# One core, local plus downsampled attention feeding two expert layers: the first batch's attention in another order, other warm-up thresholds, other scatter costs in the build-time planner

## The chip, the cores and the metric

The kernel runs on one core of a Trainium2 chip. The core has five engines with instruction queues of their own, each worked off strictly in the order written: TensorE (PE; its weight loads, PEld, overlap its matmuls), VectorE (DVE), ScalarE (ACT), GpSimd (POOL) and SyncE (SP), which here only issues DMA transfers. The metric is the device time of one execution in microseconds (us), smaller is better. Engines meet through semaphores: an instruction at the head of a queue that waits for another engine holds up all that stands behind it.

## The reference

```python
# attention: q, k, v are (4 batches, 8 heads, 576 tokens, 64)
q_d = q.reshape(B, H, Sd, 4, D).mean(axis=3)      # k_d, v_d alike: 144 tokens
out_d = sm_attn(q_d, k_d, v_d)                    # softmax attention, downsampled
out_up = np.repeat(out_d, 4, axis=2)
mask = np.abs(pos[:, None] - pos[None, :]) < 4    # a band of 7 keys
out_local = softmax(where(mask, scale * q @ k.T, -1e9)) @ v
x = (out_up + out_local)                          # to (2304 tokens, 512)
# expert 1: 512 -> 2048 -> 512
h = x @ w_in; g = maximum(h, 0) + alpha * minimum(h, 0); x = g @ w_out
# expert 2: 512 -> 2048 -> 512
h = x @ w_in; g = where(h > 0, h, exp(minimum(h, 0)) - 1); y = g @ w_out
```

## The kernel before

**Work.** The eight heads of a batch are handled as four pairs (p = 0 to 3), and a batch's tokens as two halves (u = 0, 1) of 288. For batch 0 the local part is computed with dense matmuls over blocks of 64 queries by 70 keys: `th_dense(p, u)` adds the mask (`maskb,identb` on the PE), makes the scores (`qk,qk 64x70`), takes the row maximum (`Dmx`), exponentiates (`dP`), divides (`Dden`), transposes (`ident,dP`), multiplies by the values (`dP,vd`) and adds the downsampled part into the tile `x` (`p_add`). The downsampled part is a chain of its own: `th_pair(0, p)` sums q, k and v in fours on DVE and transposes the sums of v (`ident,qk`), and `th_da0(p)` makes the scores (`qk 72x144`), copies them out (`P<-bank`), takes the maximum (`dmx`), exponentiates (`P,dsum`), divides (`dsum`, then four `P<-P,dsum`), transposes (`ident,P`), multiplies by the values (`pt,qk`) and copies out (`od`).

Batches 1 to 3 go another way in their local part. For batch 1 (`th_S`, `th_soft0`, `th_p`) the scores are written to HBM (`scr<-ss`), read back along the diagonal (`s<-scr`, 72 x 32 runs of seven numbers), normalised to `a`, scattered back along the diagonal into a zeroed tensor (`pscr<-a`, pieces of 28 bytes), and read as a matrix (`pp<-pscr`), which the PE transposes (`ident,pp`) and multiplies by the values (`ppT,vb`).

**Experts.** Expert 1 walks 128 steps of one block of 128 hidden units for 288 tokens: first `mm_in` (`x,rawi` in plain fp32 for the first six steps, afterwards `xh,wi` and `xl,wi`, operands split in a high and a low part), two steps later `out1` (`r,rawo`, then `gh,wo`, `gl,wo`), whose results are evicted as `ys` and stored to HBM (`yT<-ys`). Weights come as 8-byte numbers and are decoded on ACT and DVE (`cp`, `cw`, `wi`, `wo`). Expert 2 works on blocks of 512 tokens with seven products in place of eight for a 2 by 2 split of the matrix.

**What sets the order.** The whole program is written while a planner in the kernel file runs along. Each piece of work is a generator (a thread); `spawn(thread, priority)` sorts the threads by priority, smaller first. `_Clock` keeps an assumed time of every engine and of the DMA queue. `cons()` lets the first thread go on whose next ACT, DVE or SP instruction could start about now by these times; `pe(budget)` does so for threads that want PE and free PSUM banks. The expert steps are written out in a fixed order, and attention matmuls are put between them by `tick()` and `fill()`. So a priority or an assumed cost changes nothing in what is computed: it changes which instruction stands before which, in the queue of every engine. In the first expert step the four parts of `mm_in` each wait for one pair's `x` (`run_until("xcp", kt)`).

**Warm-up matmuls.** While the planner waits, it puts in matmuls on a constant (`bank<-warm`), as long as it holds that the PE has done few columns lately: `_Clock.quiet()` compares the columns of the last four of its ticks with `WANT`.

**Names.** All instructions are recorded at one helper's line, L293 (before) or L298 (after), so a group is told by its tiles, not by its line.

Of the kernel before, what the change touches and what calls it, by code (L numbers as in the profile page):

```python
# [39 lines left out]
LAG = 2  # L40
SP_ = S + 2 * HALO
F1 = 6
G2 = 512
U2 = G2 // 2
XR = 11
# [43 lines left out]

class _Clock:  # L90
    TICK, KEEP, RISE, COLD = 2560 / 3, 2600.0, 3100.0, 12
    WANT = 4000.0, 3600.0
    LAG = {("ACT", "DVE"): 142.0, ("ACT", "PE"): 194.0, ("ACT", "SP"): 145.0, ("DVE", "ACT"): 128.0,
           ("DVE", "DVE"): 127.0, ("DVE", "PE"): 179.0, ("DVE", "SP"): 120.0, ("PE", "ACT"): 197.0,
           ("PE", "DVE"): 196.0, ("PE", "SP"): 189.0, ("DMA", "SP"): 900.0, ("DMA", "ACT"): 907.0,
# [3 lines left out]
    MANY = {"ACT": 70.0, "DVE": 93.0, "SP": 50.0, "PE": 0.0, "POOL": 90.0}  # L99

    def __init__(self):
        self.cols, self.gear = {}, []
        self.t = dict.fromkeys(("PE", "ACT", "DVE", "SP", "DMA", "POOL"), 0.0)
        self.t["SP"] = 560.0
        self.hw = 0.0
        self.ports = {"DVE": [], "POOL": []}
        self.seen = {}
        self.share = 1.0
        self.uses, self.bar, self.slots, self.count = {}, {}, {}, {}
        self.cur = self.ctx()  # L110
# [23 lines left out]

    def quiet(self):
        k = int(self.t["PE"] / self.TICK)
        return self.last(k) < self.WANT[self.fast(k)]

    def span(self, ap):
        dims = [(abs(int(a)), int(n)) for a, n in ap.ap]  # L140
# [82 lines left out]
    def dma(self, out, in_):  # L223
        outs, ins = [self.span(out)], [self.span(in_)]
        n = int(out.shape[0]) * _free(out) * (8 if out.dtype == U64 else 4)
        piece = min(self.run(out), self.run(in_))
        cost = max(n / 360 * (2 if piece < 512 else 1), n / piece / 16 * 7)
        self.t["SP"] = max(self.t["SP"], self.deps("SP", outs, ins))
        self.hw = max(self.hw + 25, self.t["SP"]) + 450
        end = max(self.t["DMA"], self.hw + 650) + cost  # L230
        self.t["DMA"] = end
        self.note("DMA", outs, ins, end)
        c = self.cur
        c["t"] = max(c["t"], end + 900)
        c["on"] = "DMA"
# [62 lines left out]
def fused_kernel(ctx: ExitStack, tc: tile.TileContext, qk, vt, vl, ql, kl, vb, w_in1, w_out1, alpha,  # L298
                 w_in2, w_out2, ident_d, mask_d, zero_d, vd, maskd_d, out):
    nc = tc.nc  # L300
    ck = _Clock()
# [1500 lines left out]
    with tc.manual_schedule():  # L1802
# [28 lines left out]
        put("vv")  # L1831
        put("vv")
        for p in range(NP):
            spawn(th_pair(0, p), -6 + p / 10)
            spawn(th_da0(p), -7 + p / 10)
            spawn(th_dense(p, 0), -9 + p / 10)
            spawn(th_dense(p, 1), US + p / 10, 0)
        spawn(th_ldw(), 0)
        for k in range(2 * NF):
# [29 lines left out]
        for s in range(NS1):  # L1869
# [36 lines left out]
            if not s:  # L1906
# [3 lines left out]
                for z in (1, 0):  # L1910
                    at(0.0)
                    SP.dma_start(out=pscr[z][0].rearrange("(q y) -> q y", y=RW + 1), in_=zero_d)
                slot[0] = 0
                spawn(th_x0(), -20)
            tm["mm", s] = ck.t["PE"]
            if s < F1:
# [125 lines left out]
```

## Time and profile before

| | |
|---|---|
| median of 3 runs | 939.83 us (933.84 to 940.98) |
| the profiled execution | 935.59 us |
| its span, first to last instruction | 933.7 us |
| outside the span | 1.9 us |
| busy in the span: PE, DVE, ACT, POOL | 97%, 77%, 56%, 0% |
| mean granted PE clock | 0.986 of full speed |

The profile comes from one execution. A busy PE is not a PE at its peak: its matmuls take twice as long while the granted clock is 0.5 (1.2 in place of 2.4 GHz). Idle time of an engine costs something only where the PE waits for it in the end, since the PE has by far the most work.

### The profile page before, as it was taken

What the parts mean: (1) busy time and instruction counts of PE and PEld (TensorE: products, weight loads), DVE (VectorE), ACT (ScalarE), POOL (GpSimd) and SP (SyncE); (2) the same over time, 40 slices, a digit from 0 to 9 for tenths busy, and PEclk for the clock granted to TensorE, in tenths of its full rate; (3) what the DMA queues carried; (4) which work ended last, traced back from release to release, by engine and by line L of the source; (5) the groups of instructions that cost most, each with busy time, mean ns of one, the idle gap of its engine ahead of it and who ended that gap; (6) DMA issues with size and microseconds to landing.
All of it is one profiled execution on the core that took longest, in us unless ns stands there. A gap on an engine that the chain in (4) does not pass through costs nothing.

```text
span 933.7 us, 17520 instructions
## 1 busy us (share of the span) xinstructions
PE 905.9 (97%) x6727; PEld 832.6 (89%) x6727; DVE 722.0 (77%) x1552; ACT 524.8 (56%) x1312; POOL 2.9 (0%) x6
## 2 busy tenths in 40 slices
PE   6899999899999999999999998999999999999998
PEld 4568998799999999999999997998989989899987
DVE  5788985436969899999536999998797659989753
ACT  5798786454444562323335676665566456756543
POOL 0000000000000000000100000000000000000000
PEclk8799999999999999999999999999999999999999
DMA  9676815414221423110203570524233243252502
GB/s 262 214 271 222 293 55 110 110 64 148 56 78 49 138 64 96 44 44 9 63 2 116 188 224 24 180 68 136 50 132 90 70 153 128 85 161 88 179 11 81
DMA packets 69417, 106.36 MB, mean 114 GB/s; under 512 B 26610, under 2 KB 43378, under 8 KB 69154
## 3 DMA queue, kind: packets, MB, share of 16 engines
q1 hardware_dynamic: 69334, 105.25, 36.3%
q8 instruction: 52, 0.85, 0.4%
q14 instruction: 31, 0.25, 0.1%
HBM read 86.89 MB, written 19.78 MB: 114 GB/s over the span
## 4 chain that ended last, share of the span: by engine, by line
PE 82%; DVE 6%; DMA 6%; ACT 4%; issue 2%; SPq 1%; DVEq 0%; ACTq 0%
PE bank L293 82%; DMA qk<-in_qk_dram 3%; DMA s<-scr 1%; SPq L293 1%; DMA pscr<-a 1%; DMA pp<-pscr 1%; DMA rawo<-in_w_out_dram 1%; DVE cw L293 1%; DVE gl L293 1%; ACT wo L293 1%; ACT n L293 1%; DVE wi L293 1%; DVE cp L293 0%; DVE r L293 0%; ACT dP L293 0%
## 5 line engine op out<-in xcount | busy, mean ns | idle before, releaser
L293 PE MATMUL bank<-gh,wo 128*128 128x288 f32 x976 | 223.7, 300 | 1.6 <-ACT ys L293 1.6
L293 PE MATMUL bank<-xh,wi 128*128 128x288 f32 x976 | 223.3, 300 | 0.0
L293 PEld LDWEIGHTS bank<-xq,wi 128*128 128x128 f32 x1536 | 195.6, 192 | 9.6 <-ACT wi L293 2.0
L293 PE MATMUL bank<-xq,wi 128*128 128x256 f32 x1536 | 198.1, 284 | 3.0 <-ACT wi L293 1.6
L293 ACT ACTIVATE n<-bank 128x288 f32<-128x288 f32 (+1 forms) x176 | 70.7, 402 | 200.1 <-PE bank L293 197.9
L293 PE MATMUL bank<-wo,gh 128*128 128x512 f32 x576 | 179.4, 393 | 0.1
L293 PEld LDWEIGHTS bank<-gh,wo 128*128 128x128 f32 x976 | 165.5, 188 | 5.8 <-issue 2.7
L293 PEld LDWEIGHTS bank<-xh,wi 128*128 128x128 f32 x976 | 164.8, 188 | 3.2 <-issue 1.7
L293 PE MATMUL bank<-gl,wo 128*128 128x288 f32 x488 | 144.7, 297 | 0.0
L293 PE MATMUL bank<-xl,wi 128*128 128x288 f32 x488 | 143.8, 295 | 0.1
L293 PEld LDWEIGHTS bank<-wo,gh 128*128 128x128 f32 x576 | 103.3, 189 | 17.8 <-ACT gh L293 0.3
L293 PE MATMUL bank<-wo,gl 128*128 128x512 f32 x288 | 112.3, 390 | 0.2 <-DVE gl L293 0.2
L293 DVE SCALAR_TENSOR_TENSOR r<-n,nal,bank 128x288 f32<-128x288 f32 x128 | 65.3, 510 | 53.6 <-ACT n L293 52.7
L293 PEld LDWEIGHTS bank<-xl,wi 128*128 128x128 f32 x488 | 92.0, 189 | 0.7 <-DVE xl L293 0.6
L293 PEld LDWEIGHTS bank<-gl,wo 128*128 128x128 f32 x488 | 91.9, 188 | 0.1
L293 ACT ACTIVATE gh<-r 128x288 fp32r<-128x288 f32 x122 | 54.0, 443 | 66.0 <-DVE r L293 65.9
L293 DVE TENSOR_TENSOR gl<-r,gh 128x288 fp32r<-128x288 f32 x122 | 55.5, 455 | 16.9 <-ACT gh L293 16.2
L293 PEld LDWEIGHTS bank<-wo,gl 128*128 128x128 f32 x288 | 54.1, 188 | 12.5 <-DVE gl L293 0.6
L293 DVE TENSOR_TENSOR gl<-n,gh 128x512 fp32r<-128x512 f32 (+1 forms) x80 | 50.5, 634 | 7.6 <-ACT gh L293 6.5
L293 DVE TENSOR_TENSOR c<-m,bank 128x256 f32<-128x256 f32 x64 | 26.7, 419 | 37.0 <-PE bank L293 36.6
L293 ACT ACTIVATE gh<-n 128x512 fp32r<-128x512 f32 (+1 forms) x80 | 46.3, 581 | 11.8 <-DVE n L293 11.6
L293 ACT ACTIVATE n<-n 128x512 f32<-128x512 f32 (+1 forms) x80 | 47.1, 589 | 2.5
(125 smaller groups left out, 1218.1 us busy)
## 6 DMA issues: line engine op xcount, KB each, us to landing
rawi<-in_w_in_dram SPq DMA_DIRECT2D x40, 512.0 KB
rawo<-in_w_out_dram SPq DMA_DIRECT2D x40, 512.0 KB
qk<-in_qk_dram SPq DMA_DIRECT2D x12, 582.0 KB
x<-yT SPq DMA_DIRECT2D x8, 576.0 KB
osp<-os SPq DMA_DIRECT2D x18, 256.0 KB
os<-osp SPq DMA_DIRECT2D x18, 256.0 KB
out_dram<-os SPq DMA_DIRECT2D x18, 256.0 KB
yT<-ys SPq DMA_DIRECT2D x28, 144.0 KB
```

The source lines that it names most:

```text
L293: return fn(*args, **kw)
```

## The change

The priorities of batch 0's first half are set by new numbers: within a pair the downsampled scores come first (-14.7), then the dense local part (-14.6), then sums and transposes (-13.3), and each pair stands a whole step of 1.0 after the one before it. Before, all four dense parts (-9) stood ahead of all four downsampled chains (-7), and these ahead of all sums (-6), a tenth apart by pair. Up to the end of the first expert step's `mm_in` the planner asks for 5600 and 5200 columns in place of 4000 and 3600 before it leaves out a warm-up matmul. And it takes a transfer in pieces under 64 bytes to cost 31 ns (into HBM) or 15 ns (else) for a piece and engine, in place of 7.

```diff
+VP = -13.3
+DP = -14.7
+NP0 = -14.6
+STEP = 1.0
...
-    WANT = 4000.0, 3600.0
+    WANT, HEAD = (4000.0, 3600.0), (5600.0, 5200.0)
...
-        return self.last(k) < self.WANT[self.fast(k)]
+        return self.last(k) < (self.HEAD if self.head else self.WANT)[self.fast(k)]
...
-        cost = max(n / 360 * (2 if piece < 512 else 1), n / piece / 16 * 7)
+        rate = 7 if piece >= 64 else 31 if out.space == bass.MemoryType.DRAM else 15
+        cost = max(n / 360 * (2 if piece < 512 else 1), n / piece / 16 * rate)
...
-            spawn(th_pair(0, p), -6 + p / 10)
-            spawn(th_da0(p), -7 + p / 10)
-            spawn(th_dense(p, 0), -9 + p / 10)
+            spawn(th_pair(0, p), VP + p * STEP)
+            spawn(th_da0(p), DP + p * STEP)
+            spawn(th_dense(p, 0), NP0 + p * STEP)
...
                 slot[0] = 0
+                ck.head = False
                 spawn(th_x0(), -20)
```

No instruction is added or taken away on ACT, DVE, POOL and SP; on the PE the warm-up matmuls go from 27 to 21 (17 ahead of the first score and 10 between the pairs, now 18 and 3). All else is order. Three places show it.

The PE's queue after the second pair's dense scores, before the change. `dP_188`, `dP_220` and `dP_245` are the probabilities of the dense parts of pairs 0, 1 and 2; `qk_31` is pair 3.

```order
L293 MATMUL bank_73<-ident,dP_188 70x128 x4
L293 MATMUL bank_66<-ident,dP_188 70x128
L293 LDWEIGHTS identb
L293 MATMUL bank_67<-maskb,identb 128x350
L293 MATMUL bank_67<-qk_31_133,qk_30_132 64x70 x10
L293 LDWEIGHTS identb
L293 MATMUL bank_67<-maskb,identb 128x350
L293 MATMUL bank_68<-ident,dP_220 70x128 x4
L293 MATMUL bank_69<-ident,dP_220 70x128
L293 MATMUL bank_73<-ident,dP_245 70x128 x4
L293 MATMUL bank_66<-ident,dP_245 70x128
L293 MATMUL bank_72<-qk_11_117 72x144
```

The same place now; `qk_01` and `qk_11` carry the sums of pairs 0 and 1, `dP_189` and `dP_236` the dense parts of pairs 0 and 1.

```order
L298 MATMUL bank_72<-qk_11_117 72x144
L298 MATMUL bank_73<-qk_11_117 72x144
L298 MATMUL bank_67<-ident,qk_01_108 72x128 x2
L298 LDWEIGHTS identb
L298 MATMUL bank_68<-maskb,identb 128x350
L298 MATMUL bank_68<-qk_21_125,qk_20_124 64x70 x10
L298 LDWEIGHTS identb
L298 MATMUL bank_68<-maskb,identb 128x350
L298 MATMUL bank_66<-ident,P 72x72 x4
L298 MATMUL bank_72<-ident,P 72x72 x4
L298 MATMUL bank_73<-ident,dP_189 70x128 x4
L298 MATMUL bank_69<-ident,dP_189 70x128
```

Pair 1's downsampled scores (`qk_11_117`) and pair 0's downsampled transposes (`ident,P`) moved ahead of the dense work of pairs 2 and 3.

The end of this stage on the PE, before: from the last product but one of the downsampled chains to the end of the first expert step's four parts (`x,rawi`, three and one).

```order
L293 MATMUL bank_68<-pt,qk_20_124 64x144 x4
L293 MATMUL bank_67<-ident,P 72x72 x4
L293 MATMUL bank_73<-ident,P 72x72 x4
L293 MATMUL bank_66<-dP_245,vd_138 64x64 x8
L293 MATMUL bank_66<-dP_245,vd_138 64x32 x2
L293 MATMUL bank_69<-pt,qk_30_132 64x144 x4
L293 MATMUL bank_70<-x,rawi_280 128x288 x3
L293 MATMUL bank_72<-dP_291,vd_140 64x64 x8
L293 MATMUL bank_72<-dP_291,vd_140 64x32 x2
L293 MATMUL bank_70<-x,rawi_280 128x288
```

And now.

```order
L298 MATMUL bank_70<-x,rawi_275 128x288 x2
L298 MATMUL bank_66<-pt,qk_20_124 64x144 x4
L298 MATMUL bank_69<-ident,P 72x72 x4
L298 MATMUL bank_72<-ident,P 72x72 x4
L298 MATMUL bank_67<-ident,qk_31_133 72x128 x2
L298 MATMUL bank_68<-dP_299,vd_138 64x64 x8
L298 MATMUL bank_68<-dP_299,vd_138 64x32 x2
L298 MATMUL bank_73<-pt,qk_30_132 64x144 x4
L298 MATMUL bank_70<-x,rawi_275 128x288
L298 MATMUL bank_66<-dP_355,vd_140 64x64 x8
L298 MATMUL bank_66<-dP_355,vd_140 64x32 x2
L298 MATMUL bank_70<-x,rawi_275 128x288
```

The first two expert parts now stand ahead of pair 2's downsampled product; pair 3's chain still comes last.

SP's queue around batch 1's way through HBM, before. `pscr_96` and `pscr_97` are the scattered probabilities of the two halves.

```order
L293 DMA s_1876<-scr_0_94 72x32x7
L293 DMA scr_1_95<-ss 72x624
L293 DMA pscr_96<-a 72x32x7
L293 DMA yT_82<-ys 128x288 x2
L293 DMA s_1973<-scr_1_95 72x32x7
L293 DMA pp<-pscr_96 72x624 x2
L293 DMA yT_82<-ys 128x288 x2
L293 DMA qk<-in_qk_dram 128x1164
L293 DMA vv<-in_vt_dram 128x576
L293 DMA pp<-pscr_96 72x624
L293 DMA pscr_97<-a 72x32x7
L293 DMA pp<-pscr_96 72x624
```

And now.

```order
L298 DMA s_1874<-scr_0_94 72x32x7
L298 DMA scr_1_95<-ss 72x624
L298 DMA yT_82<-ys 128x288 x2
L298 DMA s_1969<-scr_1_95 72x32x7
L298 DMA pscr_96<-a 72x32x7
L298 DMA yT_82<-ys 128x288 x2
L298 DMA qk<-in_qk_dram 128x1164
L298 DMA vv<-in_vt_dram 128x576
L298 DMA pscr_97<-a 72x32x7
L298 DMA pp<-pscr_96 72x624 x2
L298 DMA qk<-in_qk_dram 128x1164
L298 DMA vv<-in_vt_dram 128x576
```

The first scatter moved behind the first two stores of `yT` and the second read of scores, and all reads of scattered probabilities moved behind the second scatter. In the PE's queue the first `ident,pp` moved from behind 486 expert matmuls to behind 564.

## Rows read from the trace of the kernel before

**Rows 1.** The page: the span, busy time of each engine.

```profile
span 933.7 us, 17520 instructions
PE 905.9 (97%) x6727; PEld 832.6 (89%) x6727; DVE 722.0 (77%) x1552; ACT 524.8 (56%) x1312; POOL 2.9 (0%) x6
```

**Rows 2.** The chain that ended last, 0 to 90 us: start, length, what.

```profile
29.19 0.67 DVE dmx L293
...
30.15 1.70 ACT P L293 x8
...
45.88 0.47 DVE x L293
...
46.40 22.34 PE bank L293 x200
```

**Rows 3.** Windows: PE, PEld, DVE, ACT, POOL busy; granted PE clock; DMA share, GB/s.

```profile
28.00:32.00 4.00, 1.75 (x20) 1.09 (x17) 3.08 (x11) 2.67 (x12) 0.00 (x0) 0.90 1.06 243
32.00:36.00 4.00, 3.81 (x37) 3.15 (x38) 1.95 (x8) 3.17 (x14) 0.00 (x0) 0.50 0.92 235
44.00:48.00 4.00, 3.44 (x47) 2.10 (x46) 3.14 (x8) 2.18 (x4) 0.00 (x0) 0.89 0.22 84
```

**Rows 4.** Waits of the PE, 46 to 130 us: for what, us in total, times, longest.

```profile
PE bank L293 <- DMA qk<-in_qk_dram: 1.6, 2, 0.9
PE bank L293 <- DMA rawo<-in_w_out_dram: 1.2, 1, 1.2
PE bank L293 <- DVE x L293: 0.6, 1, 0.6
```

**Rows 5.** The same, 130 to 300 us.

```profile
PE bank L293 <- DMA pp<-pscr: 3.0, 3, 1.7
PE bank L293 <- ACT ys L293: 1.6, 1, 1.6
```

**Rows 6.** The same, 490 to 580 us.

```profile
PE bank L293 <- ACT wi L293: 1.6, 1, 1.6
PE bank L293 <- DVE wi L293: 1.3, 1, 1.3
```

**Rows 7.** Timeline of the PE, 0 to 60 us: start, busy, operation, [idle before].

```profile
26.18 0.72 PE L293 MATMUL bank<-pt,qk 72*64 72x144 f32 x8
...
29.60 0.72 PE L293 MATMUL bank<-qk 64*72 64x144 f32 x8
32.20 1.51 PE L293 MATMUL bank<-pt,qk 72*64 72x144 f32 x8 [1.88 <-ACT pt L293]
...
36.75 1.24 PE L293 MATMUL bank<-pt,qk 72*64 72x144 f32 x8
37.91 1.18 PE L293 MATMUL bank<-ident,P 72*72 72x72 f32 x8
39.02 1.28 PE L293 MATMUL bank<-dP,vd 70*64 70x64 f32 x20
...
41.99 3.14 PE L293 MATMUL bank<-x,rawi 128*128 128x288 f32 x6 [0.66 <-DVE rawi L293]
```

**Rows 8.** The chain that ended last, 130 to 185 us.

```profile
152.00 5.19 DMA s<-scr
...
160.57 7.51 DMA pscr<-a
...
168.16 5.86 DMA pp<-pscr
```

**Rows 9.** Timeline of ACT, 130 to 185 us.

```profile
156.00 0.71 ACT L293 ACTIVATE ys<-bank 128x288 f32<-128x288 f32 x2 [2.24 <-DMA yT<-ys]
```

**Rows 10.** Timeline of the PE, 128 to 185 us.

```profile
158.43 0.70 PE L293 MATMUL bank<-ident,pp 72*78 72x72 f32 x8
```

**Rows 11.** Timeline of SP's queue, 130 to 185 us.

```profile
149.22 0.30 SPq L293 DMA_DIRECT2D pscr<-a  x1
151.01 0.82 SPq L293 DMA_DIRECT2D yT<-ys  x2
```

More of the change, by code (lines that the diff above doesn't have):

```diff
@@ L101, in __init__ @@
     def __init__(self):
-        self.cols, self.gear = {}, []
+        self.cols, self.gear, self.head = {}, [], True
         self.t = dict.fromkeys(("PE", "ACT", "DVE", "SP", "DMA", "POOL"), 0.0)
```

## The prediction

> **What bounds the kernel now.** First the page's busy times: the PE works 905.9 of 933.7 us [rows 1], so all but 27.8 us of the span is PE work that this change doesn't touch, and only the idle time of the PE and its time at half clock can be won. Then the chain that ended last, for the place of both. In the first 46 us it runs over loads, DVE and ACT; from 46.40 it is 22.34 us of PE without a break [rows 2]. So everything ahead of 46.40, the start of the last part of the first expert step, is a lead that the whole kernel pays. Then the windows for the clock: from 32 to 36 the PE is busy 3.81 of 4.00 us, but at a granted clock of 0.50, 1.2 in place of 2.4 GHz. The mean of 0.90 in 28 to 32 puts the fall at 31.2, and the 0.89 in 44 to 48 the rise at 44.9 [rows 3]. Last the PE's waits behind the lead, by what ended them: 3.4 us from 46 to 130 [rows 4], 4.6 from 130 to 300 [rows 5], 2.9 from 490 to 580 [rows 6]. The sum is made against the profiled execution's 935.59, of which 1.9 lies outside the span. It is one of the lower of the four times shown; the median lies 4.2 higher.
>
> **The lead.** ACT, DVE and the PE do the same work in both kernels, apart from warm-ups, and the first loads come in the same order. What changes is what still has to run when the last pair's probabilities are ready. Before, four dense parts went first and the downsampled chains came one after another, so that their transposes and products piled up behind 32.2 and ran at half clock. Now pairs 0 and 1 are through before pair 2's chain begins. I walked the new queues by hand, with the durations of the rows. Pair 2's exponentials stand on ACT behind pair 3's dense ones and the copies for pair 1, and start at an estimated 28.4 (30.15 before), taking 1.70 [rows 2]. Behind them come two pairs of copies (0.65 each), the maximum (0.67 [rows 2], 1.2 with its scaling and hops) and pair 3's exponentials, which so end at an estimated 35.1; two more copies make it 36.2. From there the PE has, at half clock, a product `pt,qk` (1.24), transposes `ident,P` (1.18), the transposes of v's sums (an estimated 0.64), `dP,vd` (1.28), `pt,qk` (1.24), one expert part (3.14 / 6 = 0.52) and `dP,vd` (1.28) [rows 7]: 7.4, so 43.6. The last add (0.47 [rows 2]) and two hops of 0.15 put the last part of the first expert step at 44.4, 2.0 ahead of 46.40.
>
> Against it stands the clock. In the kernel before it rose at 44.9, 2.9 us after the expert parts had begun in a row at 41.99 [rows 7], and so ahead of the unbroken stretch. Now two parts run early, between small matmuls, and the dense stretch begins only at 44.4. If it takes the clock 2.9 us again, 1.45 us of work are lost there. Net I take **0.6**. Upward: a fall only at 31.2, as before, would by the same walk give 43.3, so 3.1 - 1.5 = 1.6; no fall at all is a rival below. Downward: the walk sums some thirty short instructions and may be 2 off, so -1.4.
>
> Will it fall? The planner now wants more columns, but sees fewer gaps in its own order and puts in 3 warm-ups between the pairs, not 10. My walk leaves the PE idle for about 2 us near 25 (for the copy `pt` of pair 1 behind the dense exponentials) and 1.5 near 30. Before, it had been idle only since 30.3 (29.60 + 0.72) when the clock fell at 31.2 [rows 3, 7], among the same small matmuls. That is the nearest row, so I take it that the clock falls between 24 and 28. The Trainium skill, page "TensorE: Matmul & The Clock Gate", section "Why this matters for your kernels", speaks for the other side: it asks only that no long idle gaps stand between bursts of matmuls, and by that the clock would hold here. The trace doesn't bear it out for this mix, since 0.9 us of idle time was enough. By the rule the sum would be that of the first rival.
>
> **From 46 to 130.** The loads of batch 1's q and k stand one place earlier on SP, and the score matmuls of its second pair now stand behind 126 expert matmuls, not 105. Of the 1.6 us that the PE waited for `qk` [rows 4] I take **1.0** as won. The waits for `rawo` and `x` lose no cause. The bounds are all 3.4, and -2.2: one weight load of 512 KB slips behind the stores of `yT0a`, into a stretch with fuller queues, and takes 2.2 at the 243 GB/s of [rows 3]; ACT and DVE decode at high load there, but that weight (block 10 of `w_in`) is needed only in the eleventh step of the next group, which hides it. Without that cover the 2.2 would be paid.
>
> **From 130 to 300.** Two causes. First, the stores of `ys`: the first scatter was issued at 149.22 and the first two stores at 151.01 [rows 11] went behind it, so ACT waited 2.24 for a free `ys` tile until 156.00 [rows 9], and the PE 1.6 for a bank [rows 5]. Now the stores stand ahead of the scatter: 1.6 is won. Second, the reads `pp`: the PE waited 3.0 for them [rows 5]. The first transposes `ident,pp` stood at 158.43 [rows 10]. They now stand behind 78 more expert matmuls, at 905.9 / 6727 = 0.135 each [rows 1] 10.5 us, and some 1.5 us of other attention work moved ahead: 158.4 - 1.6 + 12.0 = 168.8 on the old scale. The price is that SP waits for the second half's probabilities before it issues any read. The second read `s` was issued at 152.00 and took 5.19 [rows 8] behind the first scatter; ahead of it, some 1.5 less. So the second scatter goes out near 159, not 160.57, and the first reads right behind. A scatter took 7.51, a read behind it or behind the loads of q, k and v 5.86 [rows 8]. If the scatter holds them up wholly, they land near 159 + 7.5 + 2 = 168.5, just in time. Each later read starts when a transpose frees its tile, 4 to 6 us ahead of its own turn. I take **4.0** of the 4.6 as won, with bounds of 0 and 4.6.
>
> The Trainium skill, page "DMA: Bandwidth & Descriptors", section "Queues, rings and completion order", says that an engine takes descriptors in ring order and that a transfer's completion is written only after all earlier writes of that engine. By it every read behind the second scatter is late; no row shows a read that overtook a scatter, and 5.86 fits. By the rule the sum would be that of the second rival, if later reads lose as much.
>
> **From 490 to 580.** DVE and ACT prepare `wo` earlier and some `wi` later by a place or two. It can take away the 2.9 us or double them [rows 6]; the moves go both ways, so I count 0. The remaining order differs between attention and expert work that the PE's queue hides.
>
> **Sum:** 0.6 + 1.0 + 4.0 = 5.6, and 935.6 - 5.6 = **930.0**.
>
> **Rivals.** *The clock holds* through the lead. Then the seven PE pieces shrink by 0.72 / 1.24 [rows 7], from 7.4 to 4.3, pair 3's scores come 1.1 earlier, and the last part starts at 40.5: 5.9 in place of 0.6, and 924.7. For it: the PE's gaps are filled better than before. Against it: seven warm-ups fewer, and the fall at 31.2 after less than a microsecond of idle time.
>
> *The reads stay late.* Each read lands 5.86 after its issue, behind scatter and loads, while its tile comes free only about 4 us ahead of its turn. Four such misses of 1 to 1.5 us eat up the 4.6: 935.6 - 0.6 - 1.0 = 934.0. For it: all reads now stand behind both scatters. Against it: they have 10 us more.
>
> *The low clock lasts* (the slower side). Behind 44.4 the PE alternates expert parts with the second half's dense scores. If this mix did not raise the clock, the 22.34 us stretch [rows 2] would run at half speed. Each low microsecond loses half of one; from 14 us on (14 / 2 = 2.0 + 1.0 + 4.0) the kernel is slower than before, and with the whole stretch it is 935.6 - 7.0 + 22.3 = 951. Against it: in 44 to 48 the same kinds of matmul held the full clock [rows 3].
>
> That the change doesn't do what its words say is true for the warm-ups (21, not more than 27), and lies in the forecast.
>
> **How the numbers follow.** Chances: forecast 0.45, clock holds 0.25, reads late 0.23, low clock lasts 0.07. The range: 922 takes in the first rival with 2.7 us of luck in the open terms; 938 takes in the second, with the 4.2 us by which the median of the runs lies over the profiled one. Only the third falls out, and tails. About 1%, 9.4 us, is what a measurement of this kernel can tell from no change. The forecast's gain of 5.6 stays within it, unless the open terms add 4 (a third of its 0.45); the first rival's 10.9 goes beyond. So faster 0.25 + 0.15 = 0.40, slower 0.06, within 0.54.
>
> **What would show it.** Right: the last `x,rawi` of the first step between 43 and 45; a clock of 0.50 from before 30 to about 47; no wait for `ys` and under 1 us for `pp`. Wrong in the lead: a clock of 1.00 from 20 on, and the last `x,rawi` by 41. Wrong in the middle: several waits for `pp` behind 168. The forecast fails altogether if the PE gains waits for `wi` near 560, or for weights before 130.

## The result and the profile after

The changed kernel takes 927.48 us (median of four runs, 925.15 to 928.21), the kernel before beside it 940.4. The ratio is 0.9875 with a 95% interval of 0.9838 to 0.9912, so the change makes the kernel 1.25% faster. The profiled execution took 928.21 us against a forecast of 930.0 and against 935.59 before; its span is 7.3 us shorter. By the medians the gain is 12.9 us, because the profiled execution of the kernel before was one of its shorter ones.

The page's head: the span and the busy times, to be held against [rows 1].

```profile
span 926.4 us, 17510 instructions
PE 903.6 (98%) x6721; PEld 831.4 (90%) x6721; DVE 721.1 (78%) x1552; ACT 523.3 (56%) x1312; POOL 2.9 (0%) x6
```

The PE's busy time fell by 2.3 us and its idle time by 5.0. Its timeline in the lead, with the idle time before each row in brackets, answers [rows 7].

```profile
22.08 0.46 PE L298 MATMUL bank<-qk 64*72 64x144 f32 x2
24.60 0.71 PE L298 MATMUL bank<-qk 64*72 64x144 f32 x6 [2.05 <-ACT od L298]
26.38 1.52 PE L298 MATMUL bank<-pt,qk 72*64 72x144 f32 x8 [1.07 <-ACT pt L298]
...
33.86 1.24 PE L298 MATMUL bank<-x,rawi 128*128 128x288 f32 x4 [0.24 <-DVE rawi L298]
35.92 0.72 PE L298 MATMUL bank<-pt,qk 72*64 72x144 f32 x8 [0.82 <-ACT qk L298]
...
38.90 0.75 PE L298 MATMUL bank<-x,rawi 128*128 128x288 f32 x2
39.58 0.78 PE L298 MATMUL bank<-dP,vd 70*64 70x64 f32 x20
41.39 0.75 PE L298 MATMUL bank<-x,rawi 128*128 128x288 f32 x2 [1.03 <-DVE x L298]
```

The last part of the first expert step starts at 41.39 us, 5.0 earlier than the 46.40 of [rows 2]. Two of its four parts already stand at 33.86. Two new waits of 2.05 and 1.07 us stand before 26.4, both for ACT. The windows of the same stretch (PE, PEld, DVE, ACT and POOL busy, granted clock, DMA share, GB/s) tell what they did to the clock, as [rows 3] did.

```profile
24.00:28.00 4.00, 2.33 (x15) 1.67 (x16) 1.68 (x6) 3.84 (x18) 0.00 (x0) 0.77 1.03 410
28.00:32.00 4.00, 4.00 (x36) 3.04 (x36) 3.19 (x11) 3.05 (x13) 0.00 (x0) 0.50 1.06 288
32.00:36.00 4.00, 2.94 (x20) 2.03 (x20) 2.52 (x9) 3.68 (x15) 0.00 (x0) 0.88 0.89 316
```

A mean of 0.77 puts the fall to half clock at 26.2, the 0.88 the rise at 33.0. So the low stretch, which lay on 31.2 to 44.9 before [rows 3], ends ahead of all expert parts. What ACT was doing while the PE stood shows in ACT's timeline.

```profile
20.42 0.40 ACT L298 ACTIVATE qk<-bank 72x256 f32<-72x256 f32 x1
23.70 0.66 ACT L298 ACTIVATE cp<-rawi 128x512 f32<-128x512 f32 x1 [2.89 <-DMA rawi<-in_w_in_dram]
24.27 0.28 ACT L298 ACTIVATE od<-bank 128x144 f32<-128x144 f32 x1
...
25.91 0.71 ACT L298 ACTIVATE pt<-bank 72x288 f32<-72x288 f32 x2
```

ACT stood 2.89 us at `cp`, the first step of decoding the first weight block, until that block had landed. The copy `od`, pair 3's dense exponentials and the copy `pt` queued behind it, and the PE waited for these.

In the middle the PE's waits from 130 to 300 us, the view of [rows 5], are nearly gone.

```profile
PE bank L298 <- DVE wi L298: 0.6, 1, 0.6
PE bank L298 <- DMA qk<-in_qk_dram: 0.3, 1, 0.3
```

The queue of SP around batch 1's way through HBM (start, time on the queue) and the first transposes of what it reads answer [rows 10, 11].

```profile
148.61 2.22 SPq L298 DMA_DIRECT2D pscr<-a  x1
150.88 2.20 SPq L298 DMA_DIRECT2D yT<-ys  x2
...
156.55 0.32 SPq L298 DMA_DIRECT2D pscr<-a  x1
157.24 3.02 SPq L298 DMA_DIRECT2D pp<-pscr  x2
```

```profile
165.96 0.67 PE L298 MATMUL bank<-ident,pp 72*78 72x72 f32 x8
167.31 0.69 PE L298 MATMUL bank<-ident,pp 72*78 72x72 f32 x8
```

The reads go out right behind the second scatter, 8.7 us ahead of their transposes, which start without a wait.

A ledger tells where the time came from. It takes the start of ACT's copy `n<-bank` of an expert step in the profiled execution of before (its start there is given), less the start of the same copy in another run. The runs e1 to e12 are those of the next section; the second column is the start of the last part of the first expert step (43.60 is read as the last `x,rawi` of that step), the third the stretch at half clock in the lead from 20 us on, worked out from the windows' means as above.

| run | last part | half clock | 47.2 | 148.5 | 291.6 | 464.4 | 866.2 |
|---|---|---|---|---|---|---|---|
| before | 46.40 | 31.2-44.9 | 0 | 0 | 0 | 0 | 0 |
| after | 41.39 | 26.2-33.0 | 4.2 | 3.9 | 9.1 | 9.1 | 7.2 |
| e1 | 41.77 | 23.7-33.9 | 3.8 | 3.4 | -3.3 | -3.7 | -4.2 |
| e2 | 46.28 | 30.2-50.6 | -0.5 | -2.3 | 1.3 | 0.5 | 0.1 |
| e3 | 43.10 | 35.5-49.2 | 2.5 | -0.6 | 4.5 | 4.0 | 4.8 |
| e4 | 42.25 | 25.6-46.1 | 3.3 | 2.3 | 7.5 | 4.7 | 4.4 |
| e5 | 43.60 | none | 2.9 | 4.2 | 2.5 | 2.5 | 1.1 |
| e6 | 42.52 | none | 3.0 | 2.6 | 7.3 | 6.8 | 6.1 |
| e7 | 40.70 | 27.1-30.6 | 4.9 | 4.8 | 10.0 | 9.9 | 9.4 |
| e8 | 41.40 | 23.8-34.0 | 4.2 | 4.0 | 8.6 | 9.3 | 7.6 |
| e9 | 40.68 | 23.7-34.0, 41-44 | 4.9 | 4.1 | 9.0 | 8.2 | 9.2 |
| e10 | 38.13 | none | 7.4 | 6.9 | 12.0 | 12.2 | 12.2 |
| e11 | 40.53 | 24.8-35.0 | 5.0 | 4.5 | 2.3 | 1.2 | -0.9 |
| e12 | 40.57 | none | 5.0 | 4.5 | 9.7 | 9.7 | 9.5 |

Two steps of the ledger need care. At 47.2 the new order of the lead has 21 more matmuls of the second half behind it than the old one, and at 148.5 eight products `pt,vs` (0.65 us) still ahead; at the later steps both orders have done the same work. So the lead is read at the last part. In the changed kernel 5.0 us are won there, 1.1 of them are lost again up to 148, 5.2 are won from 148 to 292, and 1.9 are given back late. In idle time of the PE: 5.0 us between the first two steps for 2.85 before, and 0.1 between 148 and 292 for 4.7 before.

Ahead of 20 us the clock was at half speed once more in six of the executions (10.7 to 17.6 before, 12.5 to 19.3 after, also in e2, e5, e6 and e9), and not in the others. The changed kernel and e8 differ in it and agree from the scores at 24.60 to the last part (41.39 and 41.40), so it cost nothing there.

### The profile page after: what moved, and what is told of

It is laid out like the page before. It is cut to its first block, busy times and chain, and to the rows that moved or that the text cites. A ratio compares the mean times of both kernels' runs of the same rounds, so it can differ in the third digit from the quotient of the medians.

```text
span 926.4 us, 17510 instructions
## 1 busy us (share of the span) xinstructions
PE 903.6 (98%) x6721; PEld 831.4 (90%) x6721; DVE 721.1 (78%) x1552; ACT 523.3 (56%) x1312; POOL 2.9 (0%) x6
## 4 chain that ended last, share of the span: by engine, by line
PE 80%; DVE 6%; ACT 6%; DMA 5%; issue 2%; SPq 0%; DVEq 0%; ACTq 0%
PE bank L298 80%; DMA qk<-in_qk_dram 2%; DMA rawi<-in_w_in_dram 1%; ACT dP L298 1%; DVE cw L298 1%; ACT wo L298 1%; DVE cp L298 1%; DVE wi L298 1%; DMA out_dram<-os 1%; ACT cp L298 1%; ACT n L298 1%; ACT cw L298 1%; ACT wi L298 1%; DVE gl L298 1%; ACT P L298 1%
## 5 line engine op out<-in xcount | busy, mean ns | idle before, releaser
L298 PEld LDWEIGHTS bank<-wo,gl 128*128 128x128 f32 x288 | 54.1, 188 | 12.5 <-DVE gl L298 0.8
L298 DVE TENSOR_TENSOR gl<-n,gh 128x512 fp32r<-128x512 f32 (+1 forms) x80 | 50.6, 634 | 9.4 <-ACT gh L298 8.5
L298 DVE TENSOR_TENSOR c<-m,bank 128x256 f32<-128x256 f32 x64 | 26.4, 419 | 36.0 <-PE bank L298 35.7
L298 ACT ACTIVATE n<-n 128x512 f32<-128x512 f32 (+1 forms) x80 | 47.2, 590 | 2.5
```

The lines of the kernel that those rows point to most:

```text
L298: return fn(*args, **kw)
```

## The experiments

Each group of four ran on one chip beside the kernel before, whose medians were 939.98 us (e1 to e4), 934.97 (e5 to e8) and 939.66 (e9 to e12). So runs of different groups are compared by their ratio to it, or by the ledger. The ratios carry the differences of the kernel before from group to group. The changed kernel is in none of the three; e9 and e8 stand for it in the third and the second.

**e1: the new priorities alone.**

```diff
-            spawn(th_pair(0, p), -6 + p / 10)
-            spawn(th_da0(p), -7 + p / 10)
-            spawn(th_dense(p, 0), -9 + p / 10)
+            spawn(th_pair(0, p), VP + p * STEP)
+            spawn(th_da0(p), DP + p * STEP)
+            spawn(th_dense(p, 0), NP0 + p * STEP)
```

> The kernel before with the twelve new priorities of the first batch alone; the transfer costs and the warm-up level stay as they were. Theory: the change consists of two independent parts, and this is the one that shortens the lead. The last part of the first expert step comes at 41.4 us as in the changed kernel (46.4 before), so about 5.0 of the 7.3 us of span are here, and the waits of 130 to 300 us (ys 1.6, pp about 3) stay: 935.6 - 5.0 = 930.6 against the profiled run of before. Rival: the order of the lead is worth only what the later order lets it keep, and with the old transfer costs the stretch 46 to 130 gives it back: within 1 us of before. Rival: all of the gain is here: 928.

Measured: 939.26 us, ratio 0.9989 (0.9967 to 1.0011). The time can't be told from the kernel before's, and the theory of two independent parts fell. The lead is won (41.77), but the middle takes more than that back: 6.8 us from 148 to 292 in the ledger. (The 8.9 of two later expectations is read between two steps around which the attention work stands differently.) Its PE timeline, and the windows there:

```profile
161.71 1.15 PE L297 MATMUL bank<-ident,pp 72*78 72x72 f32 x8 [4.46 <-DMA pp<-pscr]
...
175.07 0.38 PE L297 MATMUL bank<-ident,sm 128*72 128x128 f32 x2 [1.76 <-DVE sm L297]
```

```profile
160.00:165.00 5.00, 3.29 (x18) 3.27 (x19) 2.17 (x4) 1.11 (x3) 0.00 (x0) 0.52 0.37 99
165.00:170.00 5.00, 5.00 (x60) 4.75 (x59) 1.70 (x4) 1.68 (x4) 0.00 (x0) 0.80 1.01 74
```

The first read was issued at 156.60 and its transposes stood at 157.25, 0.7 us behind it. They waited 4.46 us, and behind that wait the clock was at half speed for some 6.8 us (0.52 and 0.80), 5.3 of them busy, which costs another 2.6. A wait of 1.02 us for `ys` at 211.5 was followed by 3.4 us more at half clock (another 1.7). With the waits for `sm` (1.8) and `ys` (1.3 in all) the PE stood idle 7.5 us between the two steps of the ledger, against 4.7 before. Idle time and low clock so make some 7.1 us, and the ledger has 6.8.

**e2: the new transfer costs alone.**

```diff
-        cost = max(n / 360 * (2 if piece < 512 else 1), n / piece / 16 * 7)
+        rate = 7 if piece >= 64 else 31 if out.space == bass.MemoryType.DRAM else 15
+        cost = max(n / 360 * (2 if piece < 512 else 1), n / piece / 16 * rate)
```

> The kernel before with the new transfer costs alone; its first 46 us are instruction for instruction those of before. Theory: the lead stays at 46.4 us, the ys wait and the pp waits of 130 to 300 us are gone, worth 4.6 us, and nothing is paid for it: 931.0. Rival: the reads' new place costs elsewhere (weights, DVE) what the waits gave, so that the time is within 1 us of before and the 4.5 us that the changed kernel gains in this stretch come from the new order of the lead.

Measured: 936.26 us, ratio 0.9950 (0.9927 to 0.9972). The lead stays (46.28) and the waits for `pp` shrink from 3.0 to 0.2. The ledger gains 3.5 between 148 and 292; the theory had 4.6. But this execution starts it at -2.3, since the clock, over the same instructions as in [rows 3], stayed low up to 50.6:

```profile
44.00:48.00 4.00, 3.44 (x27) 1.97 (x27) 2.56 (x6) 1.06 (x4) 0.00 (x0) 0.50 0.23 92
48.00:52.00 4.00, 4.00 (x47) 2.93 (x48) 2.61 (x7) 2.66 (x13) 0.00 (x0) 0.67 1.08 356
```

e1 wins nothing that can be told from zero and e2 0.5%, both together 1.25%: the parts don't add up. With the old order the costs are worth 3.5 us between 148 and 292, with the new order 12.0 (5.2 in place of -6.8).

**e3: 27 fillers in the two waits of the changed lead.** `fill_pe(n)` issues n warm-up matmuls outside the planner's book, so that nothing moves.

```diff
             for r in range(2):
+                if (b, p, i, r) == (0, 2, 0, 1):
+                    fill_pe(18)
                 PE.matmul(out=bks[r][0:72, i * SD:(i + 1) * SD],
...
         vs = st["vs", key[0], key[1]]
+        if key[:2] == (0, 1):
+            fill_pe(9)
```

> The changed kernel with 18 more warm-up matmuls inside its wait of 2.05 us at 24.6 and 9 more inside the one of 1.07 us at 26.4, and nothing moved. It tells what the low clock costs there. Theory: the clock falls because TensorE stands still from 22.5 to 26.4, so with the places filled it is 1.00 through 24 to 36 us; the 6.9 us of pieces between 26.4 and 33.3 become 3.5 to 4, ACT and the vector engine are next, and the last part comes at 39.5 instead of 41.4: 926.3 against 928.2. Rival: the clock holds, but the pieces only wait longer for ACT, since the exponentials and copies of pairs 2 and 3 were the limit: last part within 0.5 us of 41.4 and the time the same. Rival: the fillers hold the clock only up to 28 and it falls again: same.

Measured: 929.94 us, ratio 0.9889 (0.9863 to 0.9916). The second rival was right on the mechanism, and a little too mild: the clock held to 35.5, then fell over the expert parts.

```profile
33.20 1.24 PE L298 MATMUL bank<-x,rawi 128*128 128x288 f32 x4 [0.92 <-DVE rawi L298]
35.26 1.03 PE L298 MATMUL bank<-pt,qk 72*64 72x144 f32 x8 [0.82 <-ACT qk L298]
...
43.10 1.33 PE L298 MATMUL bank<-x,rawi 128*128 128x288 f32 x2 [0.56 <-DVE x L298]
```

At full clock through 26 to 33 the first expert parts came only 0.66 us earlier (33.20 for 33.86), and 0.22 of that is the first weight block, whose copy `cp` ACT began at 23.48 for 23.70. So the low stretch there is cheap: ACT and DVE set the pace. From 35.5 on it is dear, and the last part came 1.7 later.

**e4: the first weight block issued earlier**, ahead of the last five `vd`.

```diff
...
+        raw[1, "i", 0] = wp.tile([128, 512], U64, tag="wi0", name="rawi0")
+        nc.sync.dma_start(out=raw[1, "i", 0], in_=w_in1[0])
         at(0.0)
         load_vd(NP - 1, 0)
```

> The changed kernel with one transfer issued earlier: the first block of w_in ahead of the last five vd transfers instead of behind them, every other instruction in its place. Theory: ACT's early copy cp of that block stands 2.9 us for it (20.8 to 23.7) with od, the exponentials of pair 3 and pt behind it, and this is what makes TensorE wait 2.05 and 1.07 us. Issued near 11 instead of 16.3 the block lands some 3 to 4 us earlier, ACT's wait falls below 0.5, TensorE's two waits together below 1, and the last part comes 2.5 to 4 us earlier, the more if the clock now holds by itself: 924 to 926. Rival: the DMA engines are full from 12 to 36 us, the block lands at 22 or later and what waited for ACT waits for it still: less than 1 us. Rival: the lead shortens but the work behind 50 us waits for the weights that come at their old time: within 1 us of the changed kernel with a last part before 40.

Measured: 931.31 us, ratio 0.9907 (0.9882 to 0.9931), no gain. Half of the theory holds: ACT's copy started at 19.89 without a wait. But ACT next stood for the first block of `w_out`, and the clock fell at 25.6 and stayed low over all four expert parts.

```profile
19.89 0.74 ACT L298 ACTIVATE cp<-rawi 128x512 f32<-128x512 f32 x1
...
25.06 0.68 ACT L298 ACTIVATE cp<-rawo 128x512 f32<-128x512 f32 x1 [1.37 <-DMA rawo<-in_w_out_dram]
```

The first parts came at 31.98, 1.9 earlier, the last at 42.25, 0.9 later. Behind that, a wait of 1.5 us for `qk` near 295 with a clock of 0.83 in 290 to 300 took 2.8 in this execution.

**e5: fillers in the lead of the kernel before**, 52 by the same helper.

```diff
+        if not key[0]:
+            fill_pe({1: 4}.get(key[1], 0))
...
+        if not key[0]:
+            fill_pe({1: 16, 2: 8}.get(key[1], 0))
...
+                if not f:
+                    fill_pe({0: 18, 3: 6}.get(kt, 0))
```

> The kernel before with 52 more warm-up matmuls inside TensorE's idle places of the lead (4 and 16 ahead of pieces of pair 1, 8 ahead of pair 2's weighted sums, 18 and 6 ahead of two parts of the first expert step), nothing moved. It tells how much of the lead's 46.4 us in the kernel before is the clock and how much the order. Theory: order first. The weight blocks are decoded late there (ACT's first cp at 39.4 us, 23.7 in the changed kernel), so with the clock at 1.00 throughout the first part still waits for the decode until near 41.3 and the last part comes at 44.6: of the 5.0 us that the changed kernel gains, 1.8 are the clock's and 3.2 the order's; time about 2 us under before's. Rival: clock first. The last part comes at 42 or earlier, and the order is worth 1 us or less. Rival: the fillers do not hold the clock (0.50 again from 33): the same time as before.

Measured: 930.23 us, ratio 0.9953 (0.9936 to 0.9970). The clock was 1.00 from 20 to 60, and the last part came at 43.60:

```profile
40.66 1.62 PE L293 MATMUL bank<-x,rawi 128*128 128x288 f32 x6
...
43.60 0.70 PE L293 MATMUL bank<-x,rawi 128*128 128x288 f32 x2
```

That is 2.8 us earlier. This execution stood 0.4 ahead already when the low stretch of the other began to matter (`pt,qk` at 31.83 for 32.20), so the low clock cost the old lead 2.4 us, between theory (1.8) and rival (4.4 or more). The first part still waits for the weights' decode, as the theory had it: 40.66 against 41.99.

**e6: 73 fillers in the changed lead**, through to the last expert part.

```diff
+                    fill_pe({2: 30}.get(p, 0))
...
+            fill_pe({1: 9, 2: 7}.get(key[1], 0))
...
+                fill_pe({3: 10}.get(p, 0))
...
+                    fill_pe({0: 8, 3: 9}.get(kt, 0))
```

> The changed kernel with the idle places of its lead filled to the end of the first expert step (73 warm-up matmuls: 30, 9, 10, 8, 7 and 9), where the run before with 27 held the clock only to 35.5 us and then lost it over 15 us of expert parts. Theory: what counts is where the low stretch lies, not whether there is one: in the changed kernel it covers 26 to 33, where full clock gave only 0.7 us. With the clock at 1.00 from 20 to 50 the last part comes at 40.5 instead of 41.4 and the run is 1 us under the changed kernel: 926 to 927. Rival: it falls again behind the last filler, between 40 and 45, over expert parts: 2 to 4 us over the changed kernel.

Measured: 928.28 us, ratio 0.9921 (0.9899 to 0.9943). The clock was 1.00 from 18 us on, but the last part came only at 42.52. The PE's timeline and ACT's show where that was lost:

```profile
21.60 3.54 PE L463 MATMUL bank<-warm 128*128 128x256 bf16 x30
26.17 0.71 PE L298 MATMUL bank<-qk 64*72 64x144 f32 x6 [1.03 <-ACT od L298]
```

```profile
25.27 0.66 ACT L298 ACTIVATE cp<-rawi 128x512 f32<-128x512 f32 x1 [4.78 <-DMA rawi<-in_w_in_dram]
```

The 30 fillers ended at 25.14, and the scores behind them waited another 1.03 us for the copy `od`. That stood on ACT behind `cp`, which began 1.57 us later than in the changed kernel (25.27 for 23.70), since the first weight block landed later in this execution (its transfer was issued at 16.74, ahead of all these fillers); the scores came 1.57 later too (26.17 for 24.60). So it is the load that took the theory's 40.5, and not, as the expectation of e12 has it, fillers that outlasted their wait. From `cp` to the last part it is 17.25 us here and 17.69 in the changed kernel. e12 repeats it with fewer fillers.

**e7: e4 with fillers in what waits it left** (17 and 7, 13, 12 and 9).

> The earlier transfer of the first weight block and fillers in every idle place that it left (58 warm-up matmuls). With the earlier transfer alone ACT's wait went from 2.9 to 1.4 us (now for the first block of w_out) and the first expert part came at 32.0 instead of 33.9, but the clock was 0.50 from 27 to 46 and the last part came at 42.3. Theory: the clock took the gain away. Held at 1.00, the last part comes at 38.5 to 39.5, 2 to 3 us ahead of the changed kernel, and the run at 925 to 926, below both kernels. Rival: the parts behind it wait for the weights' decode, which starts no earlier than before: last part at 40.5 and the time within 1 us of the changed kernel. Rival: the clock falls all the same, at or behind the last filler: 929 to 931.

Measured: 926.26 us, ratio 0.9904 (0.9884 to 0.9925). The last part came at 40.70, near the rival's 40.5, with the clock low only from 27.1 to 30.6 and ACT standing 2.01 us for the first block of `w_out`. On the same chip it is 2.5 us below e8, whose lead is the changed kernel's.

**e8: only the cost of small pieces written.**

```diff
-        rate = 7 if piece >= 64 else 31 if out.space == bass.MemoryType.DRAM else 15
+        rate = 31 if piece < 64 and out.space == bass.MemoryType.DRAM else 7
```

> The changed kernel with the new transfer cost for small pieces written to DRAM only (31 ns); small pieces read back cost 7 ns again instead of 15. It tells which of the two numbers keeps the 130 to 300 us free of waits with the new order of the lead (with neither of them that order lost 8.9 us between 158 and 240 and had waits for pp of 4.5, for sm of 1.8 and for ys of 1.3). Theory: the stores to scr and pscr are the ones that the planner had taken too short, so this half is enough: no pp wait over 1 us, and the time within 2 us of the changed kernel. Rival: the reads of pp and s come too early in the queue without their own cost and hold up qk and the stores: a pp or sm wait of 2 us or more stays, 931 to 936.

Measured: 928.72 us, ratio 0.9930 (0.9912 to 0.9948); the profiled execution took 927.81, the changed kernel's 928.21. The theory holds by the waits and the ledger. (The changed kernel's ratio was 0.9875, but beside it the kernel before took 940.4, and here 934.97.) Its waits from 130 to 300 us are these, and no `pp`:

```profile
PE bank L298 <- DVE wi L298: 0.6, 1, 0.6
PE bank L298 <- ACT ys L298: 0.3, 1, 0.3
```

Here the first reads go out ahead of the second scatter, at 155.09, and their transposes stand at 160.16, 5.1 us behind.

**e9: without the higher warm-up level**, one warm-up matmul fewer.

```diff
-    WANT, HEAD = (4000.0, 3600.0), (5600.0, 5200.0)
+    WANT = 4000.0, 3600.0
...
-        return self.last(k) < (self.HEAD if self.head else self.WANT)[self.fast(k)]
+        return self.last(k) < self.WANT[self.fast(k)]
```

> The changed kernel without the third part of the change, the higher level for warm-ups up to the first expert step; what differs is one warm-up matmul of the first five microseconds. Theory: this part does nothing; the time is the changed kernel's within 1.5 us, and the run serves as its time on this chip, beside the next ones. Rival: the one warm-up moves the point at which the clock falls in the lead, and the time moves by 2 us or more with it.

Measured: 927.63 us, ratio 0.9887 (0.9864 to 0.9911): the changed kernel's time. This part does nothing that can be told from zero.

**e10: the first blocks of `w_in` and `w_out` both issued earlier, 43 fillers** (16 and 6, 8, 6 and 7).

```diff
         nc.sync.dma_start(out=raw[1, "i", 0], in_=w_in1[0])
+        raw[1, "o", 0] = wp.tile([128, 512], U64, tag="wo0", name="rawo0")
+        nc.sync.dma_start(out=raw[1, "o", 0], in_=w_out1[0])
```

> As the run with the earlier first weight block and the filled idle places, with the first block of w_out issued earlier as well (ACT stood 2.0 us for it at 23.8 there) and fewer fillers (43 for 58: those ahead of the last exponentials' transposes and of the first expert part had outlasted the wait by about 0.7 us each). Theory: the copies of pair 2's sums, their maxima and exponentials hang on ACT there, so they come 1.5 to 2 us earlier, and the last part comes at 38.5 to 39.2 instead of 40.7; the time is 1.5 to 2 us below that run, 3 to 4 below the changed kernel. Rival: the decode of the weight blocks on the vector engine, which ran without a pause from 34 to 43.7, is the next bound: last part 39.7 to 40.3, half a microsecond won. Rival: the vd transfers that now come later hold up the weighted sums: nothing won.

Measured: 924.80 us, ratio 0.9848 (0.9821 to 0.9874), 2.8 us below e9 on the same chip and the fastest kernel of the study. ACT no longer stands for a weight block, and the last part comes at 38.13:

```profile
20.00 0.74 ACT L298 ACTIVATE cp<-rawi 128x512 f32<-128x512 f32 x1
...
23.68 0.69 ACT L298 ACTIVATE cp<-rawo 128x512 f32<-128x512 f32 x1
```

```profile
30.59 1.24 PE L298 MATMUL bank<-x,rawi 128*128 128x288 f32 x4 [0.25 <-DVE rawi L298]
...
38.13 0.75 PE L298 MATMUL bank<-x,rawi 128*128 128x288 f32 x2
```

That is 2.4 us ahead of e12, with the clock at 1.00 in both: as much as ACT's copy of the `w_out` block comes earlier (23.68 for 26.10).

**e11: only the cost of small pieces read.**

```diff
-        rate = 7 if piece >= 64 else 31 if out.space == bass.MemoryType.DRAM else 15
+        rate = 15 if piece < 64 and out.space != bass.MemoryType.DRAM else 7
```

> The changed kernel with the new transfer cost for small pieces read from DRAM only (15 ns); small pieces written cost 7 ns again instead of 31. The run with the other half alone had the changed kernel's time and no pp wait. Theory: it is the stores that had been planned too short, so without their cost the new order of the lead loses most of 8.9 us again between 158 and 240, with a pp or sm wait of 2 us or more: 933 to 937 on the scale of the changed kernel's 928. Rival: either half alone delays the reads enough: within 2 us of the changed kernel.

Measured: 934.09 us, ratio 0.9944 (0.9919 to 0.9969). The theory holds, with the wait and the low clock of e1:

```profile
161.33 1.18 PE L298 MATMUL bank<-ident,pp 72*78 72x72 f32 x8 [3.71 <-DMA pp<-pscr]
```

```profile
160.00:165.00 5.00, 3.67 (x23) 3.62 (x24) 2.34 (x5) 1.81 (x5) 0.00 (x0) 0.63 0.86 168
165.00:170.00 5.00, 5.00 (x51) 4.54 (x51) 2.65 (x6) 0.45 (x2) 0.00 (x0) 0.69 0.50 75
```

The read went out at 156.64 and its transposes stood at 157.62.

**e12: 49 fillers in the changed lead, sized to its waits** (18; 8 and 5; 8; 3 and 7, at the places of e6).

> The changed kernel with 49 fillers, sized to its waits (18, 8, 8, 3, 5 and 7): in the run with 73 the clock was 1.00 throughout, but the first 30 outlasted their wait and put everything behind them 1.5 us later. It gives the lead of the new order at full clock, against 43.6 us for the last part in the old order at full clock. Theory: last part at 40.5 to 41, so the new order is worth 2.6 to 3.1 us where the clock does not differ, and the low stretch of 26 to 33 in the changed kernel cost it under 1 us: time within 1 us of the changed kernel. Rival: at full clock the two orders differ by less than 1.5 us (last part at 42 or later): the change won its lead by moving the low stretch, and not by its order.

Measured: 927.37 us, ratio 0.9890 (0.9863 to 0.9917), e9's time within 0.3 us. The clock was 1.00 throughout, and:

```profile
33.04 1.24 PE L298 MATMUL bank<-x,rawi 128*128 128x288 f32 x4 [0.59 <-DVE rawi L298]
...
40.57 0.75 PE L298 MATMUL bank<-x,rawi 128*128 128x288 f32 x2
```

The theory holds: 3.0 us between the two orders at full clock (43.60 - 40.57), and under 1 that the low stretch cost the changed lead. Of the 0.8 between the last parts (41.39 - 40.57) the first weight block has one half: ACT began its `cp` at 23.32 for 23.70. From there to the last part it is 17.25 us here and 17.69 in the changed kernel, so the low stretch cost 0.4. The 3.0 holds for a block that comes as early as that; in e6, also at full clock, it came at 25.27, and 1.1 were left.

## Why the prediction was right, and where it wasn't

The forecast of 930.0 was 1.8 us above the profiled execution and 2.5 above the median: faster, by a little more than foreseen. Its sum of 5.6 stands against 7.4. That they lie so close is in part luck, since large errors cancel: the lead gave 5.0 where 0.6 was forecast and the middle 5.2 for 4.0, while the stretch up to 148 lost 1.1 where 1.0 was to be won, and 1.9 were lost late, where nothing was forecast. Of the signs that the prediction named, the one for the middle came true; the one for the lead (the last `x,rawi` between 43 and 45, half clock to about 47) didn't.

**The lead** was the mis-sized term: 0.6 forecast, 5.0 measured at the last part. The walk itself came out close. (The terms that it names add up to 34.3, and not to 35.1, for the end of pair 3's exponentials; the trace has 35.0. Those of the rival of a clock that holds give 40.2, not 40.5.) The seven PE pieces behind it began at 35.92, for 36.2. The step that failed is the clock over these pieces, and with it "If it takes the clock 2.9 us again". The fall between 24 and 28 was right. But the clock rose at 33.0, at the end of 6.6 us of small matmuls without a break from 26.38 on (before, 9 us of them from 32.20 had not raised it [rows 7]), and not behind the dense expert parts. So the seven pieces took 4.4 us (35.92 to 40.36) and not 7.4, and the 1.45 us were not lost: together the 4.4 that were missing.

What the order and the clock are worth apart, e5 and e12 tell. At full clock the order alone is worth 3.0; the low stretch cost the old lead 2.4 and the new one 0.4, so 3.0 + 2.4 - 0.4 = 5.0. (e5 and e12 both stood 0.4 ahead of the profiled execution of their kernel before the low stretch, which leaves the 3.0 as it is.) So the low stretch parts the changed kernel from one at full clock by 0.4 us, and not by the 4 that the rival of a clock that holds gave it. The Trainium skill, page "TensorE: Matmul & The Clock Gate", section "Why this matters for your kernels", asks for no long idle gaps between bursts; with the waits filled the clock was indeed 1.00 from 20 to 52 in e5, e6, e10 and e12. That 0.9 us of idle time was "enough" for a fall is not borne out as a rule: ahead of the last part the changed kernel, e1, e8, e9 and e11 all wait 1.03 or 1.04 us, and the clock fell there in e9 alone.

The walk gave the idle place near 25 only half of its cause. It named the copy `pt` behind the dense exponentials; these stood themselves behind `cp`, which waited 2.89 us for the first weight block. e10 shows the price: 2.4 us of lead. The 1.5 us of idle time near 30 did not come; the PE was busy throughout 28 to 32.

**From 46 to 130** 1.0 was forecast, and 1.1 were lost up to 148. New waits took the place of those of [rows 4]:

```profile
PE bank L298 <- ACT dP L298: 1.8, 2, 0.9
PE bank L298 <- DMA qk<-in_qk_dram: 1.3, 1, 1.3
PE bank L298 <- ACT ys L298: 1.3, 1, 1.3
```

The bounds of -2.2 and 3.4 held. What failed is that only a weight load was set against the new order, and not these waits.

**From 130 to 300** 4.0 was forecast and 5.2 measured between 148 and 292; the PE's busy time in the 170 us rose from 165.28 to 169.41. The mechanism was right: the stores of `ys` went ahead of the scatter, and the reads had landed when the PE came to them. The stores go ahead in e1 and e8 as well, and there a wait of 0.3 for `ys` is left of the 1.6. The rival of late reads failed; it read the lateness off the reads' place behind the second scatter, and what decided was how far they were ahead of their transposes: 8.7 and 5.1 us without a wait (after, e8), 0.7 and 1.0 with 4.5 and 3.7 us of it (e1, e11). (Before, 2.7 were enough: the first read went out at 155.77, its transposes stood at 158.43 [rows 10]. So a read does not always take as long.) The Trainium skill, page "DMA: Bandwidth & Descriptors", section "Queues, rings and completion order", has a completion written only after all earlier writes of its engine, by which each read behind the scatter would be late. They may have been; if so, 8.7 us hid it, and no run here separates the two. Of the two new numbers the one for written pieces is enough (e8), the one for read pieces is not (e11).

**From 490 to 580** nothing was forecast and nothing came: the PE waits 1.6 for ACT's and 1.3 for DVE's `wi` as in [rows 6].

**What the sum left out.** It took lead and middle as terms that add. e1 shows that they don't: the earlier lead, with the old transfer costs, moves the transposes up against the reads and takes 6.8 us longer than the kernel before from 148 to 292. The lead's gain reaches the end only with the new costs. Left out too are the 1.9 us given back late. 1.2 of them were lost near 770 us in this execution, which has waits of 0.6 us for DVE there; e8, e9 and e12 have none, and their ledger ends at 7.6, 9.2 and 9.5. So the late loss differs between executions of one order, and can't be called the change's.

The kernel before spreads more than the changed one (933.7 to 946.5 us in one group), and its longer runs are those with the lower mean clock: 933.73 us at 0.989, 946.52 at 0.976. A straight line through its 51 runs of the three groups gives 8 us for each 0.01 of clock. The four runs of the changed kernel lie at 0.989 to 0.994. Open stays which stretches run low in the longer ones, since only one profiled execution was seen.

## What to carry to other kernels

Where a clock falls and rises again is worth more than whether it falls: ask which work lies in the low stretch, and whether another engine sets the pace there. Measure the parts of a planner's change each alone and then together, since an order that is right with one set of transfer costs can lose everything with another. When a wait names a copy on an engine that works in order, look at what that copy stood behind; here it was a decode that had been issued before its weights were in. And before a late start is put down to an edit, look up what the engine ahead of it waited for: e6's fillers looked like the cause, and a load was.

## What the runs showed that was not expected

The clock isn't set by the instructions alone. The kernel before and e2 issue the same ones up to 46 us, and were at half clock from 31.2 to 44.9 and from 30.2 to 50.6 (and, earlier, from 10.7 to 17.6 and from 13.0 to 19.9). After, e1, e8, e9 and e11 share one lead, but for a warm-up matmul, and their low stretches began between 23.7 and 26.2 and ended between 33.0 and 35.0; e9 alone fell a second time, near 41, behind a wait of 1.03 us that the others had too. Their last parts still came within 1.3 us of each other (40.53 to 41.77).

Even this spread isn't the clock's. In all five the last part starts 17.7 us (17.68 to 17.73) behind the start of ACT's `cp` of the first weight block, wherever the low stretch lies; at full clock, in e6 and e12, it is 17.25 (and 19.62 in e3, where the low stretch lies on the expert parts). What differs is when that block is in: ACT began `cp` between 22.80 (e11) and 25.27 (e6). So the landing of one load moved this lead by up to 2.5 us, and the low stretch of 26 to 33 by 0.4.

One wait in the middle of a dense kernel can be paid twice. Behind 4.46 us (e1) and 3.71 us (e11) of waiting for `pp` the clock fell to half, for about 6.8 us each time, and the work behind the wait lost another 2.6 and 3.3. The length of the wait alone doesn't decide it: behind 2.02 us (e5, to 161.18) and 1.02 us (e1, to 212.50) it fell too, behind 1.69 us (before, from 163.7) and 1.76 us (e1, to 175.07) it didn't. Behind the two waits for `wi` near 560 to 570, 1.6 and 1.3 us in every run [rows 6], it was low for 3 to 4 us in most executions, for about 7 in e8 and e11, and not at all in e3, e7 and e9.
